# Attention and a gated feed-forward layer on one core: another ending for the last block and newly searched queues

## The chip, the core and the metric

The kernel runs on one core of a Trainium2 chip. TensorE multiplies matrices into PSUM (eight banks of 128 partitions x 512 fp32), VectorE (DVE), ScalarE (ACT) and GpSimd (POOL) work on the elements, and SyncE (SP) issues the DMAs. The engines run side by side, each through a queue of its own, and wait for each other through semaphores. The metric is the device time of one execution in microseconds (us).

## The reference

x is 2048 x 512 in bf16. xn is x with each row normalised; the result is x + attention(xn) + feed-forward(xn):

```python
xn = _layernorm(x)
qkv = (xn @ wqkv)                      # 32 heads of 16
scores = einsum("bhqd,bhkd->bhqk", q, k) * 16 ** -0.5
o = einsum("bhqk,bhkd->bhqd", softmax(scores), v)
A = o.reshape(B, S, D) @ wo
gate, up = xn @ W_gate, xn @ W_up      # 512 -> 1792
B = (gate * (gate > 0) * up) @ W_down
return x + A + B
```

## The kernel before

**Blocks.** The 2048 queries are cut into four blocks of 512 (c4). The 32 heads are taken as four groups of eight (gg), each in two parts of four heads (ee). For each of the 32 triples (c4, gg, ee) the loop goes over 16 key tiles of 128 keys. A head has only 16 dimensions, so TensorE is used in pieces of 64 rows x 32 columns: four matmuls side by side in columns make a *half group* that uses one half of the rows ("row half" 0 or 1), and two half groups of different row halves can run at once. All of these matmuls are recorded at line 250, in `matmul_loaded`.

**Scores, exponentials, P V.** For most key tiles the scores go two half groups at a time, a "score pair", into one of two pairs of banks (0 and 1, 4 and 5), and ScalarE takes the exponential of both banks in one instruction (line 1375, `ring<-ps`, 718 times). For the other key tiles ("quads") the exponential is approximated by integer arithmetic: DVE adds a bias to the scores of each of four banks (line 1330) and makes two shifted copies, by DVE (line 1349) or POOL (line 1345). The products with V ("P V", `ring,v_aug` and `qd,v_aug`) are summed in PSUM over all key tiles of a triple. V has a column of ones, so the sum also gives the softmax's denominator. In all triples but the last both row halves add into one bank, and a half group that follows one of the other half in the same bank waits for it. The remaining four banks (2, 3, 6 and 7, `P_b`) serve P V sums, quads, projections and the feed-forward layer in turn.

**Normalising.** After a triple DVE copies the P V sum to SBUF, the denominators go through three small DMAs and a reciprocal, and POOL multiplies (lines 1237 and 1242); the odd part is packed into the tile of the even part by DMAs (line 1246).

**Feed-forward and output rows.** Between the score pairs TensorE does the projections, the gate and up products and the output rows. `out_rows` makes one tile of 128 output rows: 14 products with W_down, four with wo, and DVE adds the residual x and stores it through SP. For the last block the last two of the four wo products are not ready in time. `out_rows` then sums only the first 16 products, and DVE adds x to them and keeps the sum in fp32 in the space of xnT (line 1061, `resid`).

**The ending** is `normalise_last` (line 1122). For the last triple alone (`LAST2 = 1`) the two row halves of P V add into two banks, so that they need not wait for each other. When both are done, ScalarE copies the one to SBUF (line 1148) and DVE adds the other (line 1150), in two column halves; then DVE transposes (line 1153), takes the reciprocal of the denominators (line 1154), transposes these back (line 1155) and multiplies (line 1157) into `qf`. Meanwhile TensorE computes the products of wo with the two output tiles before the last for all four rows (`stream_out`, in the banks that the scores have left), and for row 3, which stands in `TAIL_ACT`, adds `resid` by an fp32 matmul with the identity (line 1133). Each row then gets its last product, from `qf`. DVE adds `resid` to rows 0 to 2 (line 1174), ScalarE copies row 3 (line 1171), and SP stores all four (line 1179). SP waits for all earlier DMAs ahead of its last `LAST_STORES` stores and for these at the end.

**What sets the order.** The kernel records 8,251 operations and an order of them is written out in `PLAN`, a packed string that a search with a planner has made beforehand: for each place in it which operation comes next, and which buffer each new tile gets. `Graph.run` unpacks it into one queue for each engine, and `Graph.emit` puts in the semaphores. The planner's costs stand in the `G.op` calls; they have no effect on the chip but through that order.

Of the kernel before, what the change touches and what calls it, by code (L numbers as in the profile page):

```python
# [13 lines left out]
ACTF = mybir.ActivationFunctionType  # L14
ALU = mybir.AluOpType

S = 2048
D = 512
H = 32
# [19 lines left out]
LAST_STORES = 4  # L39
# [15 lines left out]
LAST2 = 1  # L55
TAIL_ACT = (3,)
# [65 lines left out]
PLAN_OPS = 8251  # L122
PLAN = (
    "c-n1S1z;3c*PZibve|?P-r(+~K+zK1H53RgAq1zmLkq#JcySHx1oxuBixj8DwYa1-B)jwe``*m#&hq_5vOD|azANXP`<5z-?|)qU;npkhm-SBk%JG0+=1?9OFU$$t_)PpZ9&?`sx#E46{UQBP9-7;D"
    "=UY><D-W!Pig#D;eI!lD@z7?SVte7W#hl8mH{2Y<&EH({?qk_vJk!1JbU6Uxh2039E8-c%vSJ}9=1|2uRL+(k$TwoF?)3*vle5jk`|RXB47Z)yv>w(`bYn$sZK+tBadS6gynJfzO!nxW@#3W%C*Hxc"
    "ndc<Zc%8%A0<@vrlU5V2<p?fc$c16c1<%op4Qx@OC)|n$yk0f-l-r20y6IiHJv_N#`igVzO&o6d%sho*yJ47cl5RRc7|&g*VX%1=V+#)H9wQ*S&tK-YhNrk`mN3eg%&l{apQbZ~&E|n%_{j_vJ#(qL"
    "xrwyPo^@8V%qUxd;I?08&KMgT>sqNt&yBn^?6TZui>Y@5g?kFlc<;5*zK+~aJaj{*h+NNY#aa5(*g{w-=P8~-)6MvEFLIb$nihDA&-_ehT<qkr+8n1d`BZvZymYBzTW0KFd~TjdSf(&ru5s^CVXJcK"
    "RGMu*)0JdZ1cMn-;o>KqQhX#{x|w018>X>t=7zLNF6cIg%lU3$wtPS@nOn@43%E@ix#>g8|Gq~0;-IVnCOjz?7Uwm6&5ivm=ef<Gh!@f-Zfs{5F1%xyXyl3<z|GUjI3+9G&+s;6Qo?k%*ukwBM=-ZF"
    "wi0vQ=0@^k={C=~L}0%7*+JcljEap>JQ;75zaktfgX(6+AF;lhK4hk!6%%y0X9Rc40+Zzk6Aa8vbZ{Fncru?nDJMfNV5}iZg_&S1kL1ByGrEj}jAK^(4QowbTHE=Q1tc6v_lw%0K}im(e9#}$@j9d#"
    "w1``7W~7?P8pEZA>#Z0XhFd3>Kind}xM`)^f<422Yg5yFSjKwT!&aBx^y3~bv%#p1c;rX?KYu03UtvZ{ySZhK=@wz7=_=EcrhB+mMr7-kK$lp~JgB*pfvW%c3kq->Mwr$cCb%V6FuNKc&$!`13DZwr"  # L130
    "KoG_ln8CU7Rl+FD#z<}>V#W}zo7F9oO$Lb@Oy$98-AsF$!u2Gl;)N|w&Jd+=CSh1SW88vP4-c3&$gK^!qXW8CxjO8mDbb31M3{{%%}4O&tBXl1-Cvwv!@ZXVIJb!;?qvrb81igp{cRT^Uiwh%WNcg9"
    "qiuZFv#T|0F!!nti9lYY(CyMkx5-gUs+iDXI@wnIx)<>cZ_2eilq?s6$AhMLfK3b9>*Oo_YVHir@ja)~&EfFTY*xs=QhMe((7jY(LYqAvcI|Cty>3GtYfso5<Pk`UO|bfmvxJ0V-_S$JG6trYG$sll"
    "h2qgzoPVX6y+Jlt5WevHg0E8MD_XX3pGWg@?jxOTTE)_L7EgOnfm>{4(U3)wZtJH&U`xUnU}%)N#a+f8;<3(rgsLDqD~Q&{ZkU8?aFb*<YnBub@F6nYKofW{*VbHdPmvib7-?<DIsvN|hH?{7JhW?!"
    ";T~|em`6g1xt1Y2EtE6i%&a(WE@zzIKrZo?d|;f=l)Y|6F(sg+53YM%PV~jC_?m=fY;8<eEHPy;odt6S|H2rpc#zImSFv%wCI1bE<`z&|OUkj_FxsX2nI`KNLYs>lde#zj+)__wBA8Khd)gOce?!D6"
    "-WE&rN|txIQL@aCTZ$Juy@+byyyER3xYXfB=U_=LuBC9@t$9nq&29aOxA%}81$=5vHy{#Lhhvc|M4Bm3d^%LF*!y0Oru3Z0RQ$G+dnK`z^PU#hI+7VYGjw*KG=-1iZEk$jgGV5Fouhciac?mzwnR~M"
    "PwNU3`xR>qt6{NH5*FGk%2z<j?TxKzgSUg?RySqzGsY-xCM>t|*2f)YV+^k$rmnXT$j$(|oyiUM&_(DtcWE{U+3z|$ROZ9Ewo`E*8uvoF4Z!S|A<9={xDO0@KC!LttpM9eyo_Q2nn}1Y!9mAY*G9TW"
    "4#1OG#v)#KaZevBk>2b(J)B@#=W(h>F(f&doh41LNFL?pe&)*Hw)-d}XJn*3J9vf~lT49kp2#ki$=)P?FWm{L$$dK-#ix1o`PfFB);N1ZY>8~^uE{3Uz4^d>T6sGG+t;wfm0fb#<(iKbc7U-r$=vpo"
    "dm3@WCEUv?rg|40fL&I5FkOcY11zHER<k5A$3sz8S1a3i8?hRCiyPQ%u4qVgPy6fL$O1E1_-3)3hb0ZT<=)1@rXTSCl#}_^twXfo+@Yj+F~s^|Zsny<t0yoa-o$5%tY8N+DMj3t_HtXdZ1&SyTHiu%"
    "&yARQzr;=da_^;<mkxF7R?X;%JtPee(D}Mh_w*MQ{c+E&pA8H=O^=Zl9<^Za2W*PR7fS3&Y5=@(Il_IK4=azDM>AMGr`(;Jj*}6$dUaDc**Mo0An7=h>ukwkiyE_u4AUMvf!J=%cnV_{ohhdFGsKjU"
    ";)+Lf=$`cBp61V_eCw*vWLCMXMs}O`dL{{Zu3W9ev4U!a&$@r`5H`F-CC=xeFxwTQbq#8<w#8nyYe-8;dNhZX1G)*Ba)NGguSaAlU*FgJP?opN@=~rv!2c^CylCVBGhYc|-iTUv)0PypF`bV^+{T6}"  # L140
    "+SkNpmk!+9)Y$LrxSdXXNRs<>jMg@~?+rM&ci6V0amDvr79T@=klafQP`<L;D>FP_S$KOrPh)IAxWTDV{vUerwBPcT=dQtGeb`*4+nC<Q`d&gc?>!8($5&U<y0_uB)xEv;b!%tiX8J2y;^wyq_A5S*"
    "W$?sK_jZxo?t0yP2TNOWZo4n`Dlg+k)&3op&n3xM{LU4xLv{GveOTwyVRJUO-Q#@q6_ocH#rGCnw{A7K_5F>MBC^!2t1)g~eVG^8Ci$5cjn>Vs+um0i;A!=Q%yxmOSeI~&TNktj_>zi}&6Vf&O|fpA"
    "ty^kOZo94Coxx??HhVJKxYe}o#Ke`aX^5pbOqjPIUAI~m?g0zqytc0#yeaMZuFSZbfCtR%z-N73<i&6acHDDSZr$+dibaZ^mPhy82iaOT4+~ffWVR@V%2iCbGnmR~;e41{u{U=f3Q)kkU}q4x`Td^M"
    "xhB*Yt10;ZC8=*K!0j++YnZ@&uETu3KJ~O9%2)Vff9cbC_~ItFe+O#2jDz=EWZ&<8?f7P|GmfvAL9t!SnU`wb!&-1?C5LgdWsDPE{NF}Q@zE+i;A0e@r=o4&+xawDHstobjQyW6#+{12v-=9$^%OrJ"
    "p5WXLdR{cNU-)vLcz?~s_AA@3zht+k3IFQy+2#c$9en?L<bWgPU#O&&SrMqZs_JKpYg)h;RS!tU+fdD4eS&m&lL7u>ct*|b@2205>$$bR7@p>$XMQgFi_uRpAjJKarDyDBZq322;sJer4|##?456PG"
    "QqeXlzf|&ES)8RkaTWDhrIkR=N+&C^y|fDbq+dt^s<Q=USg5W|@4%Kv0VN!FfLsp8M@_uQ=FmR;1BChAep!D{Eth=cOmtpJNvw9H=4&8Rvijzmmk7mK*WQSBt4Hzse`&pb0ZyXcUK|?_Xbi(Av%#}~"
    "Pu=SvatqqVH^!$#_|NMb1ibY-z}fYAz<FFKjZ?2P`~-~prVRF^)!(IM<w^s?TCr7HyYGSiZC!y&R6Y7NtB7MYfOAQj^RtsioJe*$-9G?5TRK+g-IL1#2SS#+Sa(<K1z^`NwGK7-{zo8Q`=#EFT7g?1"
    "0%w~t2O0DyP(auEcPZ3=3L75@Ov%dbWq)#Z2e55k^r{xoK%EwA+Npk8b71AN4l6q?@IM3$DZp+Qxl&Y3-3eIrLfex7jMp-}OAH(ejM(#|7W7v4!$@F0-fn9&3MkeTY<=66H-NG0XY}%4azGmaOiU?t"
    "Ds`f^0_c?a$uNxD0J7%59~~FuoCY-0x+bj}j1uBisf*nML5D9h<=A$Xa~tq|&O3SU<;P~AXqkvn_-$2tQ~;ubSf5cLiLoeoF)u>UCeiUZBvCyJRPfi5aRjKg@?H>9em)FTnufHUk|+JF{tj$+rlCao"
    "_9jV1^5aC;P2EvoI`A6F9a0Le0$My;i(&V&UjjlM)gR@+ok0Eb6<`ngkN?F{lm;a99)l5+-6t#YAp<)AMSf$w=Tt^9@^Q!H!<Uo7_cG}9o&xPt{HI{Zm$mfji^}MXC`#$t!R5d##y|dY1}GmF?OHs4"  # L150
    "A<%sRdY>ugf2KklW!m?3Ci#`vN`}lvCp|!04@5v+-*!shoxo%CoSF)UY5_U!xqF-h9<=Pbd}E~g$3x`6Xss>cW&*p1Yn$Jp{lZ%L{>E`MZg`|J)xZxgvOjV8WqR#m>#HBB7RFr}_N1k!XK-r3Enu=X"
    "SNGRCP&f;^60onzF%)fe6UciK6<r;dINQ$!?mi0?Rg8MT@4fe;){<`5LCeQ1bF5~c5-K0Anm`k>1mntMRDT3y){kTC&d1r|JceJ!G5*V8l6(9m*0KT6rcjQ2(ry*Li*Kn43O+z4?PGD^C^9|S-~CPI"
    "O80=QY<MGFZ#UxXDzR36*WZO*4;Xp%Att_0Q*(W*gRdWFxliLBE?UR5<&+NRkop5I-)g;aLfF%+c)7HlwsZz?@fBvYa<j~sF@ZL?{3!EV>}cntH2YJZ?PMKU`m4zL3@w4?U5X<m3-Aw;t~zcOP=m{j"
    "8HF)jF!v|qe&j|jgtcAUQr{c^+(EV{$iQw^rNP&eg7T{wfgOPhyQRF_(0574MV)E`Eql)Dm(+|3kxuzJ^+!i5+V8dlB`&L+|2v1O=PA-ZKUw7JYP}0>Jx<fxBDt{`{#k3jx;3y<Pu7wG(P&pgY;<M6"
    "=bw(&Ox%?fbg(Z?D9`lo9T?hh4dGVwz-dcv=ezqKWdapGnr-2QihZQOHf#~;ayHV>i4dW1#$(%DtVMa?RQl&o93N<lt=QP=WVl;fH6LXEk-|8(jw)?48a};zl+_?)c>4~g%j4e={dixXX{9zu+_999"
    "b{S$=6<wp3TarqhFL#O%qjjS-(=PqD(eF#)WP;yP8|vvH<&Kx9kW4FovK-TB+i?!G&I&9RA-Y?Dzxp(e0AzE^me??f41bFiEDD5fflW3yXQT6_0Q<0N(y*nSRz6^}DTsey?N9Fz=%fg~>5M^4&F-d1"
    "trK;8t!N)YnWxo`La*Lej3rNv%X{ZcnG3rKn%X<DB>xy7QtLNIhu_ZNMAT_dWKttX<-^Iqb3~W=32g}A4o~Vn=luHCw=ayy6x|uPjmdg>c7}@Z6pmM!REnJ`<vhMeOjyzx<+pq!XpQW8;(9#L<Uj&O"
# [97 lines left out]
class Graph:  # L255
# [124 lines left out]
    def emit(self, nc, es):  # L380
# [93 lines left out]
        def play(e, eng):  # L474
# [953 lines left out]
```

## Time and profile before

| | us |
|---|---|
| median of three runs | 691.45 |
| fastest and slowest run | 690.92, 691.89 |
| profiled execution | 692.29 |
| its span, first to last instruction | 690.4 |
| busy in the span: TensorE, ScalarE, DVE, POOL | 680.9, 670.5, 603.0, 499.3 |
| first exponential starts, last one ends | 11.0, 680.45 |
| granted TensorE clock | 0.998 |

In the profile PE is TensorE, PEld its weight loads, DVE VectorE, ACT ScalarE, SPq SyncE's queue. A row of the timeline gives start, duration, engine, line, operation, what is written and read, shape and count; several like instructions are one row. A row of the stretches gives, for each engine in the order PE, PEld, DVE, ACT, POOL, its busy time and in brackets its instructions; then the granted clock, the DMA engines' busy share and GB/s; the stretches of a single tile show only the engines that touch it. A matmul's row is longer than its share of TensorE, since matmuls overlap.

### The profile page before, as it was taken

To read this page: it belongs to the slowest core of one execution; us is meant where nothing else is said; L and a number is where in the kernel's file an instruction comes from. 1 tells how busy PE (TensorE), PEld (TensorE's weight loads), DVE (VectorE), ACT (ScalarE), POOL (GpSimd) and SP (SyncE) were. 2 spreads that over 40 slices of the span, in tenths; PEclk is the share of its full clock that TensorE was granted. 3 is DMA by queue.
4 is the path that set the end of the run, shared out by engine and by line. 5 is a ranking of instruction groups with operands and counts; after the bars stand their busy time and mean duration, and the time that the engine had idled before them with its cause. 6 is when DMAs were issued, how large, how long until landed. Compare 5 with 4: busy or idle time off the path is not lost.

```text
span 690.4 us, 45217 instructions
## 1 busy us (share of the span) xinstructions
PE 680.9 (99%) x22248; PEld 357.3 (52%) x19848; DVE 603.0 (87%) x1017; ACT 670.5 (97%) x731; POOL 499.3 (72%) x507
## 2 busy tenths in 40 slices
PE   8999999999999999999999999999999999999997
PEld 4455555545545555555444565544554455555463
DVE  9958899999989788999999788989998887988876
ACT  6999999999999999999999999999999999999994
POOL 3223669777788778878677885988878778786791
PEclk9999999999999999999999999999999999999999
DMA  7330121021222021201200022030211013030111
GB/s 214 47 75 21 50 75 52 8 77 52 72 81 56 22 70 31 80 23 28 70 23 26 19 61 73 20 90 6 65 42 33 12 45 95 18 104 23 29 31 59
DMA packets 55941, 35.87 MB, mean 52 GB/s; under 512 B 19336, under 2 KB 51784, under 8 KB 55752
## 3 DMA queue, kind: packets, MB, share of 16 engines
q1 hardware_dynamic: 55752, 32.97, 17.4%
q8 instruction: 165, 2.70, 1.7%
q14 instruction: 24, 0.20, 0.1%
HBM read 26.35 MB, written 2.35 MB: 42 GB/s over the span
## 4 chain that ended last, share of the span: by engine, by line
PE 94%; DVE 4%; issue 1%; DMA 0%; POOL 0%; DVEq 0%
PE ps L250 94%; DVE qd L1330 1%; DVE stats L724 1%; DVE xn_sb L737 1%; DMA x_sb<-in_A_x_dram 0%; DVE hT L1017 0%; DVE qd L1349 0%; DVE xnT L778 0%; POOL rstd L719 0%; PE ps L1133 0%; DVE mv L725 0%; DVE xn_sb L1174 0%; DVE up_sb L1013 0%; DVE kT L866 0%; DVEq L514 0%
## 5 line engine op out<-in xcount | busy, mean ns | idle before, releaser
L1375 ACT ACTIVATE ring<-ps 128x1024 bf16<-128x1024 f32 x718 | 664.0, 1099 | 5.5 <-PE ps L250 4.1
L1345 POOL TENSOR_TENSOR qd<-qd,ints 128x512 int32<-128x512 int32 x446 | 450.0, 1039 | 157.3 <-DVE qd L1349 95.7
L250 PE MATMUL ps<-qT,kT 64*32 64x512 bf16 x8192 | 458.2, 374 | 1.0 <-DVE qd L1330 0.2
L1330 DVE TENSOR_SCALAR qd<-ps 128x512 int16<-128x512 f32 x612 | 397.8, 685 | 55.0 <-PE ps L250 50.5
L250 PE MATMUL ps<-qd,v_aug 64*32 64x512 bf16 x3672 | 267.2, 375 | 0.2 <-issue 0.2
L250 PE MATMUL ps<-ring,v_aug 64*32 64x512 bf16 x2872 | 237.7, 375 | 0.8 <-DVE kT L866 0.6
L1310 PEld LDWEIGHTS <-kT 64*32 64x32 bf16 x7676 | 156.7, 92 | 125.1 <-issue 33.0
L1282 PEld LDWEIGHTS <-v_aug 64*32 64x32 bf16 x4660 | 111.3, 91 | 70.7 <-issue 17.3
L250 PE MATMUL ps<-xnT,wgs 64*32 64x512 bf16 x1792 | 138.1, 374 | 0.3 <-issue 0.2
L250 PE MATMUL ps<-xnT,wus 64*32 64x512 bf16 x1792 | 137.8, 375 | 0.0
L808 PEld LDWEIGHTS <-wgs 64*32 64x32 bf16 x1792 | 43.3, 91 | 32.2 <-issue 8.0
L250 PE MATMUL ps<-Wd,hT 64*32 64x512 bf16 x768 | 57.7, 375 | 0.8 <-DVE qd L1330 0.7
L808 PEld LDWEIGHTS <-wus 64*32 64x32 bf16 x1792 | 43.6, 91 | 28.8 <-issue 6.2
L1349 DVE TENSOR_SCALAR qd<-qd 128x2048 int16<-128x2048 int16 x83 | 56.4, 690 | 1.9 <-PE ps L250 1.7
L808 PEld LDWEIGHTS <-hT 64*32 64x32 bf16 x1792 | 41.7, 92 | 30.1 <-issue 6.4
L250 PE MATMUL ps<-Wv,hT 64*32 64x512 bf16 x512 | 45.2, 375 | 0.0
L250 PE MATMUL ps<-Wk,hT 64*32 64x512 bf16 x512 | 43.5, 375 | 0.0
L1017 DVE SCALAR_TENSOR_TENSOR hT<-ps,up_sb 128x512 bf16<-128x512 f32 x56 | 38.4, 685 | 5.6 <-PE ps L250 5.1
L1013 DVE COPY up_sb<-ps 128x512 f32<-128x512 f32 x56 | 38.4, 685 | 3.3 <-PE ps L250 2.9
L250 PE MATMUL ps<-Wo_p,x_sb 64*32 64x512 bf16 x480 | 39.7, 375 | 0.5 <-issue 0.4
L250 PE MATMUL ps<-xnT,Wq 64*32 64x512 bf16 x480 | 36.0, 374 | 0.0
L250 PE MATMUL ps<-xnT,Wk 64*32 64x512 bf16 x480 | 34.6, 374 | 0.5 <-DVE xnT L778 0.3
(72 smaller groups left out, 266.3 us busy)
## 6 DMA issues: line engine op xcount, KB each, us to landing
rb<-rec_scr SPq DMA_DIRECT2D x31, 256.0 KB
wus<-in_B_W_up_dram SPq DMA_DIRECT2D x38, 128.0 KB, 3.1
wgs<-in_B_W_gate_dram SPq DMA_DIRECT2D x38, 128.0 KB, 3.1
xr_sb<-in_A_x_dram SPq DMA_DIRECT2D x16, 128.0 KB, 2.9
out_dram<-xn_sb SPq DMA_DIRECT2D x16, 128.0 KB, 2.2
qT<-qf SPq DMA_DIRECT2D x120, 16.0 KB, 2.8
x_sb<-in_A_x_dram SPq DMA_DIRECT2D x8, 128.0 KB, 2.4
x_sb<-oT SPq DMA_DIRECT2D x60, 16.0 KB, 2.7
```

Of the source, the lines that this page charges most:

```text
L250: return e.add_instruction(mybir.InstMatmult(name=e.bass.get_next_instruction_name(), engine=mybir.EngineType.PE, ins=[e.lower_ap(x), e.lo ...
L724: G.op("DVE", 580, lambda e, m=m: e.bn_stats(stats[:, m, :], xs(m)), reads=[t_xm[m]], writes=[t_st], prio=pr, order=last_xn if m == 4 else ())
L737: G.op("DVE", 320, lambda e, m=m, t=t_n: e.tensor_scalar(xn_sb[:, t.slot, :], xs(m), mv[:, m, 0:1], rstd[:, m:m + 1], op0=ALU.subtract, op ...
L808: e.ldweights(w()[rows, 32 * j:32 * j + 32], tile_position=(rows.start, 32 * j))
L1013: G.op("DVE", 603, lambda e: e.tensor_copy(up_sb[:, tup.slot, :], bank_of(tu)), reads=[tu], writes=[tup], prio=-590)
L1017: G.op("DVE", 603, lambda e: e.scalar_tensor_tensor(out=hT[:, th.slot, :], in0=bank_of(tg), scalar=0.0, in1=up_sb[:, tup.slot, :], op0=ALU ...
L1282: e.ldweights(vs(j), tile_position=(64 * half, 32 * j))
L1310: e.ldweights(ks(m), tile_position=(64 * half, 32 * m))
L1330: G.op("DVE", 601, lambda e, j=j, tx=tx: e.tensor_scalar(qd[:, tq.slot, 512 * j:512 * j + 512], ps[:, BANK[tx.slot], :], IBIAS[3], 0.0, op ...
L1345: G.op("POOL", POOL_NS / POOL_PIECES + 60, lambda e, x=x, n=n, c=slice(i * m, i * m + m): e.tensor_tensor(x().bitcast(I32)[:, c], raw().bi ...
L1349: G.op("DVE", 600, lambda e, n=n, x=x: e.tensor_scalar(x(), raw(), float(SHIFTS[n + 1]), None, op0=ALU.add), reads=[ti, tq], writes=[t], p ...
L1375: exp_ops[u] = G.op("ACT", 904, lambda e, tr=tr, k0=k0: e.activation(ring[:, tr.slot, :, :], ps[:, 4 * k0:4 * k0 + 2, :], ACTF.Exp, scale= ...
```

## The change

1. `LAST2 = 0`: the last triple's P V sum goes into one bank, like all others. ScalarE's two copies and DVE's two adds go; DVE transposes straight from PSUM, and its multiply reads PSUM too.
2. `TAIL_ACT = (1, 3)`: in the last block rows 1 and 3 are no longer evicted after 16 products. Their banks are kept open to the end ("held"); x is added by one more product, with the bf16 identity as weights. The last three products go into the same bank, and a shared counter (`flags`) gives the first and the last half group their marks in whatever order the queue has them. Rows 1 and 3 come after rows 0 and 2 in the sequence of jobs. The fp32 matmul is gone. Rows 0 and 2 stay as they were, in the two banks of one score pair.
3. At the end ScalarE copies rows 1 and 3 out of PSUM and issues their stores itself, with a semaphore (`stored`) for which SP waits at the very end; SP has the two stores of rows 0 and 2 (`LAST_STORES = 2`).
4. `PLAN` is new as a whole (8,248 operations), from a search whose planner lets TensorE's operations report their ends in the order of its queue. The order of all five queues differs nearly everywhere, also far from the ending.

```diff
-LAST_STORES = 4
+LAST_STORES = 2
-LAST2 = 1
-TAIL_ACT = (3,)
+LAST2 = 0
+TAIL_ACT = (1, 3)
-PLAN_OPS = 8251
+PLAN_OPS = 8248
 PLAN = (
...
+        self.stored = es.enter_context(nc.semaphore("stored"))
...
+                eng.wait_ge(self.stored, 16 * len(TAIL_ACT))
...
             t = tile or Tile("ob", P_b, BGBANKS)
+            held = c4 == NB - 1 and i in TAIL_ACT
...
+            if held:
+                pairs.append((lambda: ident[:], lambda: xr_sb[:, txr.slot, :]))
+                left = [2 * len(pairs) + 6]
+
+                def flags(n=left[0]):
+                    left[0] -= 1
+                    return left[0] == n - 1, left[0] == 0
+                mm_chain(t, pairs, reads + [txr, t_id], pr, slots=slots, flags=flags)
+                kept[i] = t, flags
+                return
...
-            for i in range(4):
+            for i in range(4) if c4 < NB - 1 else sorted(range(4), key=lambda i: i in TAIL_ACT):
...
-            tA, tB = Tile("finA", P_sc, [0]), Tile("finB", P_sc, [1])
-            rows = [(tA, 0), (tA, 1), (tB, 0), (tB, 1)]
+            free = Tile("finA", P_sc, [NU % 2])
+            rows = [(free, 0), (kept[1][0], 0), (free, 1), (kept[3][0], 0)]
...
-                    o = G.op("PE", 860, lambda e, i=i, t=t, sub=sub: e.matmul(bank_of(t, sub), identf[:], resid(i), start=False, stop=False),
...
-                G.op("ACT", 300, lambda e, c=c: e.activation(up_sb[:, tup.slot, c], at_bank(tp)[:, c], ACTF.Copy), reads=[tp],
-                G.op("DVE", 340, lambda e, c=c: e.tensor_tensor(o_sb[:, tos.slot, c], up_sb[:, tup.slot, c], at_bank(tp_hi)[:, c], ALU.add),
-                G.op("DVE", 340, lambda e, c=c: e.transpose(flip(c), o_sb[:, tos.slot, c]), reads=[to], writes=[tt] if h else [tot, tt], joins=[tot] if h else [], prio=-949 + 10 * h)
+                G.op("DVE", 340, lambda e, c=c: e.transpose(flip(c), bank(c)), reads=[tp], writes=[tt] if h else [to, tt], joins=[to] if h else [], prio=-949 + 10 * h)
...
+                G.op("DVE", 340, lambda e, c=c: e.tensor_tensor(qf[:, tl.slot, c], spread(c), bank(c), ALU.mult),
+                     reads=[ts, tp], writes=[tn] if h else [tl, tn], joins=[tl] if h else [], prio=-946 + 10 * h)
...
+                    if i in TAIL_ACT:
+                        G.op("ACT", 566, lambda e, t=t, sub=sub, to_=to_: e.activation(xn_sb[:, to_.slot, :], bank_of(t, sub), ACTF.Copy),
+                             reads=[tf, t], writes=[to_], prio=-900 + i)
+                        G.op("ACT", 100, lambda e, store=store: store(e).then_inc(G.stored, 16), reads=[to_], prio=-890 + i, name="store", lat=1900.0)
+                        continue
```

More of the change, by code (lines that the diff above doesn't have):

```diff
@@ L812, in bass_parallel_sum__mha_block__glu_gated_reglu__prompt_kernel, with mm_chain, counted @@
         chains = [0]
-        def mm_chain(tile, pairs, reads, prio, sub=0, slots=None, mode="half", weights=None):
+        def mm_chain(tile, pairs, reads, prio, sub=0, slots=None, mode="half", weights=None, flags=None):
             n = len(pairs)
             count = [0, n * (2 if mode == "half" else 1)]
-            def flags():
+            def counted():
                 count[0] += 1
                 return count[0] == 1, count[0] == count[1]
+            flags = flags or counted
             made = []
@@ L1144, in normalise_last @@
-            flip = lambda c: o_sb[:, tot.slot, c]
+                    for o in stream_out(t, sub, i, lambda tg=tg, i=i: oT_of(tg)[:, 128 * i:128 * i + 128], wo, [tg], n == 0 and i not in TAIL_ACT, False, NU + 5 + i, i not in TAIL_ACT):
+                        if i not in TAIL_ACT:
+                            o.order |= set(pv_ops[part(keys[-1])][-2:])
+            to, tup, tl = Tile("o", P_o), Tile("up", P_up), Tile("oTl", P_qf)
+            bank, flip, spread = lambda c: ps[:, BANK[tp.slot], c], lambda c: o_sb[:, to.slot, c], lambda c: up_sb[:, tup.slot, c]
@@ L1153, in normalise_last @@
[L1153 removed]
+                tt, tr, ts, tn = (Tile() for _ in range(4))
+                G.op("DVE", 340, lambda e, c=c: e.transpose(flip(c), bank(c)), reads=[tp], writes=[tt] if h else [to, tt], joins=[to] if h else [], prio=-949 + 10 * h)
                 G.op("DVE", 190, lambda e, c=c, h=h: e.reciprocal(rlast[:, 8 * h:8 * h + 8], flip(c)[:, DH - 1:256:32]), reads=[tt], writes=[tr], prio=-948 + 10 * h)
[L1155 to L1156 removed]
@@ L1157, in normalise_last @@
-                G.op("DVE", 340, lambda e, c=c: e.tensor_tensor(oTl()[:, c], o_sb[:, tos.slot, c], up_sb[:, tup.slot, c], ALU.mult),
-                     reads=[ts, to], writes=[tn], joins=[tl], prio=-946 + 10 * h)
+                G.op("DVE", 340, lambda e, c=c, h=h: e.transpose(spread(c), rlast[:, 8 * h:8 * h + 8].unsqueeze(2).to_broadcast([128, 8, 32])),
+                     reads=[tr], writes=[ts] if h else [tup, ts], joins=[tup] if h else [], prio=-947 + 10 * h)
+                G.op("DVE", 340, lambda e, c=c: e.tensor_tensor(qf[:, tl.slot, c], spread(c), bank(c), ALU.mult),
+                     reads=[ts, tp], writes=[tn] if h else [tl, tn], joins=[tl] if h else [], prio=-946 + 10 * h)
@@ L1177, in normalise_last @@
[L1177 to L1183 removed]
+                    tf, to_, m = Tile("fin%d" % i), Tile("ost", P_xn, [i]), 12 + i
@@ L1184, in stream_out @@
+                    G.op("DVE", 603, lambda e, i=i, t=t, sub=sub, to_=to_: e.tensor_tensor(xn_sb[:, to_.slot, :], bank_of(t, sub), resid(i), ALU.add),
+                         reads=[tf, t_res[m]], writes=[to_], prio=-900 + i)
+                    t.r.append(G.ops[-1])
+                    dma(store, 128, reads=[to_], writes=[Tile()], prio=NU + 20, stream=("out", m % 8))
+        def stream_out(t, sub, i, w, wo, reads, start, stop, prio, late=True):
             made = []
             for half in range(2):
-                fn, load = chain_part(w, wo, lambda: bank_of(t, sub), half, lambda first=start and not half, last=stop and half: (first, bool(last)))
+                fn, load = chain_part(w, wo, lambda: bank_of(t, sub), half, kept[i][1] if i in kept else lambda first=start and not half, last=stop and half: (first, bool(last)))
@@ L1187, in stream_out @@
                 new = not t.w
                 o = G.op("PE", 216, fn, reads=reads + [t_wo, t_wol], writes=[t] if new else [], joins=[] if new else [t], prio=prio, mode="half", half=half,
-                         bank=(t, sub), after=NU if start else None, load=load, weights=reads)
+                         bank=(t, sub), after=NU if start and late else None, load=load, weights=reads)
                 if (t, sub) in fin_prev:
```

232 lines of the change are left out of this document (98 added, 134 removed).

## The prediction

> **What bounds the kernel now.** I read the page first, then the stretches, then the timelines of each engine over the last 10 us.
>
> ```profile
> span 690.4 us, 45217 instructions
> ...
> PE 680.9 (99%) x22248; PEld 357.3 (52%) x19848; DVE 603.0 (87%) x1017; ACT 670.5 (97%) x731; POOL 499.3 (72%) x507
> ...
> L1375 ACT ACTIVATE ring<-ps 128x1024 bf16<-128x1024 f32 x718 | 664.0, 1099 | 5.5 <-PE ps L250 4.1
> ...
> L250 PE MATMUL ps<-qT,kT 64*32 64x512 bf16 x8192 | 458.2, 374 | 1.0 <-DVE qd L1330 0.2
> ```
> ```profile
> 11.00:78.00 67.00, 65.49 (x2063) 35.40 (x1970) 53.78 (x103) 65.60 (x72) 22.81 (x30) 1.00 0.32 70
> ...
> 413.00:480.00 67.00, 66.88 (x2288) 34.45 (x2008) 60.05 (x97) 67.00 (x74) 52.71 (x53) 1.00 0.18 52
> ...
> 614.00:680.50 66.50, 66.31 (x2288) 36.99 (x2004) 54.81 (x89) 65.28 (x71) 50.12 (x50) 1.00 0.14 40
> 680.50:690.40 9.90, 6.08 (x126) 1.95 (x106) 5.22 (x14) 1.25 (x3) 0.91 (x1) 0.87 0.17 55
> ```
> ```profile
> 11.00:78.00 67.00, 21.92 (x260) 65.60 (x71) 1.00 0.32 70
> ```
> ```profile
> 675.74 4.71 ACT L1375 ACTIVATE ring<-ps 128x1024 bf16<-128x1024 f32 x5
> 681.09 0.66 ACT L1148 ACTIVATE up_sb<-ps 128x256 f32<-128x256 f32 x2 [0.63 <-PE ps L250]
> 687.01 0.60 ACT L1171 ACTIVATE xn_sb<-ps 128x512 bf16<-128x512 f32 x1 [5.26 <-PE ps L250]
> ```
>
> TensorE and ScalarE run side by side and hold each other up. The 718 exponentials end at 675.74 + 4.71 = 680.45. The stretch from 413 to 480 us holds 74 of them, 0.905 us each, without idle time; the first stretch (71 of its ScalarE instructions are exponentials, by the stretches of ring alone) needs 67/71 = 0.944, the last one 66.5/71 = 0.937. So (680.45 - 11.0)/718 = 0.932 us is the mean over the middle, and 718 x (0.932 - 0.905) = 19 us are lost there, all told. Whatever the change does to TensorE's queue can give back at most these 19 us. The other 9.9 us after the last exponential are a chain of small steps:
>
> ```profile
> 680.54 0.67 PE L250 MATMUL ps<-ring,v_aug 64*32 64x512 bf16 x12
> 681.14 0.41 PE L250 MATMUL ps<-Wo_p,x_sb 64*32 64x512 bf16 x4
> 681.18 0.38 PE L250 MATMUL ps<-ring,v_aug 64*32 64x512 bf16 x4
> 681.61 1.32 PE L250 MATMUL ps<-Wo_p,x_sb 64*32 64x512 bf16 x24
> ...
> 683.60 1.12 PE L1133 MATMUL ps<-xnT,identf 128*128 128x512 f32 x2
> 684.66 0.39 PE L250 MATMUL ps<-Wo_l,x_sb 64*32 64x512 bf16 x4
> 684.69 0.38 PE L250 MATMUL ps<-Wo_l,qf 64*32 64x512 bf16 x4
> 684.88 0.38 PE L250 MATMUL ps<-Wo_l,x_sb 64*32 64x512 bf16 x4
> 685.40 1.56 PE L250 MATMUL ps<-Wo_l,qf 64*32 64x512 bf16 x28
> ```
> ```profile
> 679.96 0.68 DVE L1061 TENSOR_TENSOR xnT<-ps,xr_sb 128x512 f32<-128x512 f32 x1
> 681.63 0.75 DVE L1150 TENSOR_TENSOR o_sb<-up_sb,ps 128x256 f32<-128x256 f32 x2 [0.99 <-PE ps L250]
> 682.30 0.44 DVE L1153 STREAM_TRANSPOSE o_sb<-o_sb 128x256 f32<-128x256 f32 x1
> 682.77 0.20 DVE L1154 RECIPROCAL rlast<-o_sb 128x8 f32<-128x8 f32 x1
> ...
> 683.22 0.40 DVE L1155 STREAM_TRANSPOSE up_sb<-rlast 128x256 f32<-128x256 f32 x1
> ...
> 683.65 0.43 DVE L1157 TENSOR_TENSOR qf<-o_sb,up_sb 128x256 bf16<-128x256 f32 x1
> 684.00 0.44 DVE L1155 STREAM_TRANSPOSE up_sb<-rlast 128x256 f32<-128x256 f32 x1
> 684.47 0.42 DVE L1157 TENSOR_TENSOR qf<-o_sb,up_sb 128x256 bf16<-128x256 f32 x1
> 685.82 1.89 DVE L1174 TENSOR_TENSOR xn_sb<-ps,xnT 128x512 bf16<-128x512 f32 x3 [0.93 <-PE ps L250]
> ```
> ```profile
> L1179 SPq DMA_DIRECT2D out_dram<-xn_sb x4: 332/338/430, 686.6 to 688.1; - x4
> ...
> DMA to landing us min/median/max: 1.7/1.7/1.8
> ```
>
> The last P V group starts at 681.18 and what waits for it (DVE at 681.63, TensorE at 681.61) starts 0.43 us later: that is the price of a handover between row halves. DVE then works alone until 684.89 (both halves of qf), the first half being ready at 684.08, but TensorE is still in the fp32 matmul until 684.72 and takes it up at 684.69. Rows 0 to 2 leave through DVE from 685.82 to 687.71, row 3 through ScalarE until 687.61, but its store is issued at 688.1, behind row 2's on SP's queue. It lands about 1.8 us later, at 689.9.
>
> **The change part by part, the ending.** All times here are on the clock of before, with the last exponential at 680.45.
>
> 1. P V in one bank. In the new queue the last ring group of row half 0 stands behind nine groups of its half since the last score pair (seven before), and the waits for the packed output tile now stand among them. That makes 2 x 0.215 and up to half a microsecond of semaphore waits; I let it start at 680.9 instead of 680.54. Then row half 1 must wait for it, because both halves now add into one bank: +0.43, and five P V groups follow in series, four spacings of 0.215, the last reported 0.43 later. DVE begins at 680.9 + 0.43 + 0.86 + 0.43 = 682.6, 1.0 later than before. Best case 682.2 (no backlog), worst 683.2 (a second handover).
>
> 2. The DVE chain loses the ScalarE copies (0.66, under other work) and both adds. Two transposes, two reciprocals, then transpose, multiply, transpose, multiply: before, qf's first half came 684.08 - 682.30 = 1.78 after the first transpose and the second 2.59 after it. The operand now lies in PSUM; the nearest row that reads PSUM at this size, the add at L1150, gives 0.75 for two, against 0.43 for the multiply that reads SBUF, so I price both alike. qf is ready at 684.4 and 685.2, that is 0.3 later than before in both halves.
>
> 3. TensorE under that chain. The fp32 matmul (1.12) is gone; four half groups that add the residual by the identity come (two for each kept row, 2 x 0.215 per row half). Behind the last score pair the queue now holds 60 half groups where it held 42 and the fp32 matmul; 18 were moved there, 9 x 0.215 = 1.9 us per half. From the last P V start (682.2) eleven groups of row half 1 remain before qf is asked for, 2.4 us and some handovers: 684.7, so TensorE, not DVE, still lets the first qf group start at about the old 684.69. If this cover were longer, each group would cost 0.215.
>
> 4. The rows. Row 0 and 2 go through DVE, 1 and 3 through ScalarE, alternating. Row 0's second group follows one handover later, with two others between: its sum is there at 685.55 (before 685.80). Row 2 needs the second half of qf (685.2, start 685.4), a handover and a report: 686.25. Row 3 is last in the queue behind three groups of its half: 686.9. ScalarE takes 0.60 for it, to 687.5, and issues its store itself at 687.6 instead of SP's 688.1. Landing after 1.7 to 1.8: 689.4 instead of 689.9. DVE ends at 686.95, so row 2's store (landing 688.7) is not last.
>
> The ending gives -0.5. No DMA issued by ScalarE is in the trace. Its bounds are the landings of all stores of the output, from the view of that tensor:
>
> ```profile
> DMA to landing us min/median/max: 1.7/2.2/4.5
> ```
>
> The nearest are the four late stores at 1.7 to 1.8, on idle DMA engines as here; so I take 1.75. With the worst P V start (+0.6) and the slowest landing (+2.7) the ending costs 2.8; with the best start and no handovers left it gives 1.2. SP waits for all but its own two stores during the DVE chain and ends with one more wait for ScalarE's stores; the waits lie under the chain, and the last adds less than the 0.5 us that already follows the last landing.
>
> **The change part by part, the middle.** The order of all queues is new, from the first microseconds on; the work is the same (2,766 half groups per row half before, 2,768 after), less two DVE residual adds (L1061, 0.68 each). So I counted the queues as built.
>
> - Between two score pairs ScalarE allows 0.905 us, four groups per half (0.86) but not five (1.08). Intervals with five or more go from 111 to 105, in the last tenth from 14 to 11, which is the work moved to the end. Price of one: between 0 and 1.08 - 0.905 = 0.17; six fewer give 0 to -1.0.
> - Waits of one row half for the other at three places or less behind the awaited group: 139 before, 116 after. A place is about 670/5,650 = 0.12 us, three are 0.36, the handover 0.43; so 23 fewer save 0 to 0.1 each for most, 0 to -2.3.
> - The distances of scores to the exponential that frees their bank, and to the DVE work, are nearly the same.
>
> I take -1.2 for the middle, a little over a third of the -3.3, since ScalarE can only use what arrives at its score pairs. On the other side nothing in the counts says that the new order is worse, but a window of the old order ran at 0.937 where others ran at 0.905; were the whole middle so, it would cost 718 x 0.005 = 3.6.
>
> How the row halves start matters for all of this:
>
> ```profile
> 36.87 0.38 PE L250 MATMUL ps<-qd,v_aug 64*32 64x512 bf16 x4
> 36.88 0.38 PE L250 MATMUL ps<-Wv,xnT 64*32 64x512 bf16 x4
> 37.09 0.38 PE L250 MATMUL ps<-qd,v_aug 64*32 64x512 bf16 x4
> ...
> 37.30 0.38 PE L250 MATMUL ps<-qd,v_aug 64*32 64x512 bf16 x4
> ```
>
> In the queue all three qd groups (one half, 0.215 apart) stand ahead of the Wv group of the other half, yet this starts second. Starts run ahead by some groups. Ends are reported in order: the qf group that started at 684.69 is asked for by the one that starts at 685.40, 0.71 later and not 0.43, because the group of 684.88 stood ahead of it in the queue. The Trainium skill, page "TensorE: Matmul & The Clock Gate", section "The mechanism" in Part 3, has matmuls strictly first in, first out, in their starts and their ends; the trace agrees for the reported ends and contradicts it for the starts, and the sum goes by the trace.
>
> Sum: 692.29 (the profiled execution: span 690.4 and 1.9 around it) - 0.5 - 1.2 = 690.6. That execution stands 0.84 over the median of 691.45, so the forecast against the runs is 689.7.
>
> **The rivals.**
>
> A. Starts in queue order. Were they, a group behind one of its own half would leave the other half empty. Laid out so, the order before fills 3,100 steps of 0.215 and the new one 3,075: 25 x 0.215 = -5.4, and -0.5 for the ending: 685.6. For it: the change is to the order itself, and 19 us are there to take. Against: 36.88 above; with two groups of lead allowed, both orders come out equal to 0.1 us. The skill's rule named above would give this time.
>
> B. Slower: the score pairs of the new order come late to ScalarE, in the middle. Place: the semaphore waits of TensorE's queue, where a wait stops both halves; the new order moves nearly every one of its 5,650 groups. Price: the last window's rate, +3.6, less 0.5: 694.5. It decides from the point where the mean distance of exponentials exceeds 0.935 us (+1.9, which outweighs the ending's 0.5). For it: the windows differ that much with the same code. Against: all counts point slightly the other way.
>
> C. No difference: the ending's -0.5 is eaten by the later P V sum (worst start +0.6) and the middle stays. 691.4.
>
> **How the numbers follow.** 0.2% of 691.45 is 1.4 us, about what a measurement can tell from no change. My forecast (half of the chances, own range 687.5 to 691) is faster in four parts of five and within 0.2% in the rest: 0.40 and 0.10. A has 0.12, all faster. B has 0.25, of which 0.22 slower. C has 0.13, the same. Together: faster 0.52, same 0.26, slower 0.22. The range goes from 686.5 (most of A is out) to 693.3 (into B).
>
> **What would show it.** Right: exponentials at 0.930 us on average and the last one about 1 us earlier; after it 9.4 us instead of 9.9; DVE starting its transposes some 2.2 us after the last exponential (1.2 before for the add); first qf group at 4.2 us after it; the last store ScalarE's, landing 1.7 to 1.8 after its issue. Wrong: idle time before ScalarE's exponentials over 20 us in sum; a P V sum that ends more than 2.7 us after the last exponential; a ScalarE store that takes over 2.5 us; or a mean distance at 0.925 or less, which would be A's sign.

## The result, and the profile after

The changed kernel takes 686.5 us (median, 685.28 to 689.76) where the kernel before, run beside it, takes 691.24 (690.09 to 691.89). The ratio is 0.9938, with a 95% interval from 0.992 to 0.9956: 4.3 us less, between 3.0 and 5.5. The forecast was 689.7 us in a range from 686.5 to 693.3, so the time lies at the range's lower edge, 3.2 us below the forecast. Both steps of the forecast were wrong in size: the ending was to give 0.5 us and gave nothing, the middle was to give 1.2 and gave all of it.

The profiled execution takes 686.07 us. Its page, the lines that answer to those of before:

```profile
span 684.2 us, 45020 instructions
...
PE 675.6 (99%) x22262; PEld 345.9 (51%) x19654; DVE 598.5 (87%) x1012; ACT 666.8 (97%) x730; POOL 499.8 (73%) x507
...
L1365 ACT ACTIVATE ring<-ps 128x1024 bf16<-128x1024 f32 x718 | 660.4, 1141 | 2.9 <-PE ps L250 2.5
```

The work is the same. TensorE's busy time and the idle time ahead of the exponentials are smaller. The stretches, in the columns of before (PE, PEld, DVE, ACT, POOL):

```profile
11.00:78.00 67.00, 66.33 (x2123) 33.71 (x2022) 54.79 (x105) 66.66 (x74) 24.29 (x32) 1.00 0.32 69
413.00:480.00 67.00, 66.97 (x2269) 34.22 (x2000) 60.86 (x100) 66.98 (x74) 52.72 (x52) 1.00 0.15 40
614.00:674.25 60.25, 59.68 (x2056) 31.47 (x1768) 49.40 (x81) 60.23 (x66) 45.14 (x45) 1.00 0.13 39
674.25:684.20 9.95, 6.98 (x216) 3.32 (x180) 3.90 (x11) 1.19 (x2) 1.27 (x1) 0.96 0.18 57
```

The first stretch holds 74 ScalarE instructions where it held 72; the middle one is unchanged. The last exponential ends at 674.25 (680.45 before), and from there to the end it is 9.95 us (9.96 before). So next to nothing was won behind the last exponential. The exponentials themselves, counted by stretch, in before and after (the stretches of the tile ring; columns: length, TensorE's P V products that read ring, then the exponentials under ACT):

```profile
11.00:110.00 99.00, 33.90 (x400) 97.34 (x105) 1.00 0.29 66
110.00:540.00 430.00, 152.96 (x1864) 427.99 (x465) 1.00 0.17 46
540.00:673.00 133.00, 45.99 (x540) 131.21 (x142) 1.00 0.16 46
```
```profile
11.00:110.00 99.00, 34.47 (x416) 98.66 (x108) 1.00 0.28 66
110.00:540.00 430.00, 152.66 (x1868) 427.44 (x466) 1.00 0.17 46
540.00:673.00 133.00, 47.27 (x568) 132.98 (x146) 1.00 0.17 48
```

Three more exponentials (2.7 us at 0.905) in the first 99 us, one in the next 430 us, four in the last 133. Part of the last figure is probably chance: the kernels below with moved handovers and with joined pairs, whose order is nearly that of before, show 145 there. The profiled execution of before is also 0.84 us over its median, so the 6.2 us between these two traces are more than the 4.3 us between the kernels.

The ending of after, DVE, ScalarE and the stores:

```profile
676.94 0.78 DVE L1151 STREAM_TRANSPOSE o_sb<-ps 128x256 f32<-128x256 f32 x2 [2.67 <-PE ps L250]
...
678.32 0.42 DVE L1155 TENSOR_TENSOR qf<-up_sb,ps 128x256 bf16<-128x256 f32 x1
...
679.13 0.42 DVE L1155 TENSOR_TENSOR qf<-up_sb,ps 128x256 bf16<-128x256 f32 x1
```
```profile
680.88 0.37 ACTq L1162 DMA_DIRECT2D out_dram<-xn_sb  x1
681.35 0.60 ACT L1164 ACTIVATE xn_sb<-ps 128x512 bf16<-128x512 f32 x1 [0.51 <-PE ps L250]
681.98 0.34 ACTq L1162 DMA_DIRECT2D out_dram<-xn_sb  x1
```
```profile
DMA to landing us min/median/max: 1.7/1.8/2.0
```

And TensorE, from the last score pair on:

```profile
672.74 0.38 PE L250 MATMUL ps<-xr_sb,ident 64*32 64x512 bf16 x4
673.46 0.41 PE L250 MATMUL ps<-Wo_p,x_sb 64*32 64x512 bf16 x4 [0.34 <-issue]
673.51 0.38 PE L250 MATMUL ps<-Wd,hT 64*32 64x512 bf16 x4
673.67 0.41 PE L250 MATMUL ps<-ring,v_aug 64*32 64x512 bf16 x4
...
675.18 0.41 PE L250 MATMUL ps<-ring,v_aug 64*32 64x512 bf16 x4
...
679.05 0.59 PE L250 MATMUL ps<-Wo_l,qf 64*32 64x512 bf16 x8
```

The first Wo_p group (row 1's product with the packed output tile) carries 13 semaphore waits, and it starts 0.72 us after the group ahead of it in its half, which is 0.51 more than the usual spacing of 0.215; the profile shows 0.34 of it as idle time of the whole engine. The last ring group comes at 675.18, 0.93 us after the last exponential. DVE starts its transposes at 676.94.

### The profile page after: what moved, and what is told of

It reads as the page before. It is cut to its first block, busy times and chain, and to the rows that moved or that the text cites. A ratio compares the mean times of both kernels' runs of the same rounds, so it can differ in the third digit from the quotient of the medians.

```text
span 684.2 us, 45020 instructions
## 1 busy us (share of the span) xinstructions
PE 675.6 (99%) x22262; PEld 345.9 (51%) x19654; DVE 598.5 (87%) x1012; ACT 666.8 (97%) x730; POOL 499.8 (73%) x507
## 3 DMA queue, kind: packets, MB, share of 16 engines
q8 instruction: 164, 2.69, 1.6%
## 4 chain that ended last, share of the span: by engine, by line
PE 75%; ACT 18%; DVE 5%; issue 1%; DMA 0%; POOL 0%; ACTq 0%
PE ps L250 75%; ACT ring L1365 18%; DVE stats L726 1%; DVE qd L1320 1%; DVE xn_sb L739 1%; DVE v_aug L876 0%; DMA x_sb<-in_A_x_dram 0%; DVE qT L952 0%; DVE mv L727 0%; ACT xn_sb L1164 0%; DVE qd L1339 0%; DVE xnT L780 0%; POOL rstd L721 0%; DVE xnT L1075 0%; DVE kT L869 0%
## 5 line engine op out<-in xcount | busy, mean ns | idle before, releaser
L250 PE MATMUL ps<-qT,kT 64*32 64x512 bf16 x8192 | 448.7, 374 | 1.3 <-DVE qd L1320 0.4
L250 PE MATMUL ps<-qd,v_aug 64*32 64x512 bf16 x3672 | 263.0, 375 | 1.1 <-issue 0.9
L1300 PEld LDWEIGHTS <-kT 64*32 64x32 bf16 x7584 | 151.1, 92 | 126.6 <-issue 32.6
L1272 PEld LDWEIGHTS <-v_aug 64*32 64x32 bf16 x4544 | 108.7, 91 | 75.6 <-issue 20.4
L250 PE MATMUL ps<-xnT,wus 64*32 64x512 bf16 x1792 | 136.4, 374 | 0.0
L810 PEld LDWEIGHTS <-hT 64*32 64x32 bf16 x1792 | 40.2, 92 | 28.2 <-issue 4.2
```

Of the source, the lines that this page charges most:

```text
L250: return e.add_instruction(mybir.InstMatmult(name=e.bass.get_next_instruction_name(), engine=mybir.EngineType.PE, ins=[e.lower_ap(x), e.lo ...
L810: e.ldweights(w()[rows, 32 * j:32 * j + 32], tile_position=(rows.start, 32 * j))
L1272: e.ldweights(vs(j), tile_position=(64 * half, 32 * j))
L1300: e.ldweights(ks(m), tile_position=(64 * half, 32 * m))
```

## The experiments

Two theories stood against each other. *Order*: the gain is the new order of the middle alone. *Ending*: the order can be looser because the new ending takes work out of the last stretch (18 half groups moved behind the last score pair, two DVE adds gone). All edits of order below move operations in the written-out order and leave everything else as it is.

**The changed kernel again**, to stand beside three of the others.

> The changed kernel once more, unedited, so that it stands beside the three others on one chip. Both theories: 0.9938 of the kernel before, between 0.992 and 0.9956, as measured.

685.26 us, ratio 0.9941 (0.9923 to 0.9959). From the last exponential to the end 9.88 us.

**The order without the ending, and the ending without the order.** The first pair was joined at the 660th exponential:

```diff
 before.py
-PLAN: order of before
+PLAN: order of after up to score pair 660, from there the order of before (buffers renamed to fit)
```

> The kernel before, ending and all, but with the changed kernel's order of work for everything up to the 660th exponential; from there on the order of before. Order theory (the gain is the order of the middle, and the ending is worth nothing): the two traces stand about 5.1 us apart at the 660th exponential (4.67 at the 648th, 5.51 at the 672nd), so 691.2 - 5.1 = 686.1 us, between 685.2 and 687.2. Ending theory (the order can be looser because the ending takes work out of the last stretch): the gain does not come over, 690.5 to 691.5 us.

> The mirror image: the changed kernel, new ending and all, but with the order of before up to the 660th exponential. Order theory: only what the traces gained behind the 660th exponential is left, 6.2 - 5.1 = 1.1 us, so 691.2 - 1.1 = 690.1 us, between 689.3 and 691.2. Ending theory: as the changed kernel, 686 to 687.5 us.

689.02 us, ratio 0.9991 (0.9982 to 0.9999), and 694.97 us, ratio 1.0072 (1.006 to 1.0084). Taken as they are, both numbers speak against the order theory. The trace of the first shows why they can't be taken so. Up to the 660th exponential it runs 5.13 us ahead of the profile of before (after: 5.36). Behind the seam ScalarE stands still twice (timeline of ScalarE), and TensorE's waits in the same stretch name GpSimd:

```profile
625.80 6.60 ACT L1375 ACTIVATE ring<-ps 128x1024 bf16<-128x1024 f32 x7 [1.26 <-PE ps L250]
633.74 2.85 ACT L1375 ACTIVATE ring<-ps 128x1024 bf16<-128x1024 f32 x3 [1.34 <-PE ps L250]
```
```profile
PE ps L250 <- POOL qd L1345: 2.4, 2, 1.5
```

At that place 16 operations stand on different sides of the cut in the two orders, a quad's shifted copies on GpSimd among them, so the joined order has them late. The pair was repeated with a cut at the 633rd exponential, where only two DMA issues differ:

> The kernel before with the changed kernel's order up to the 633rd exponential, joined where only two of the 8,251 steps stand on different sides of the seam (both DMA issues; at the 660th it was 16 steps, GpSimd's pieces of a row group among them, and the trace lost 2.8 us right behind the seam). Order theory: what the traces had gained by there, 4.35 of 6.27 us, 69% of the whole gain of 4.3 us, so 3.0 us less than before (ratio 0.9957, between 0.994 and 0.9975). Ending theory: no gain, ratio 0.999 to 1.001.

> The changed kernel with the order of before up to the 633rd exponential, the same clean seam. Order theory: the 31% of the gain that came behind that point, 1.3 us less than before (ratio 0.998, between 0.9965 and 1.0). Ending theory: all of the gain, ratio 0.9938.

686.89 us, ratio 0.9956 (0.994 to 0.9972), and 687.95 us, ratio 0.9979 (0.9968 to 0.9989). Both fall on the order theory's numbers (0.9957 and 0.998), and the ending theory's lie outside both intervals. The exponentials by stretch, of the first and of the second:

```profile
11.00:110.00 99.00, 34.34 (x412) 98.38 (x107) 1.00 0.27 65
```
```profile
11.00:110.00 99.00, 33.71 (x400) 97.33 (x105) 1.00 0.27 67
```

The early gain goes with the order, not with the ending. Of the whole, 0.0044/0.0062 or some 70% comes ahead of the 633rd exponential without any part of the new ending. The other 30% comes with the new ending and the order around it, but ahead of the last exponential: the tail is 9.96 us in the one and 9.98 in the other. Which of the two earns those 30% these runs don't tell.

**Parted score pairs.** In before 40 score pairs have another half group between their two halves in TensorE's queue; in after two have.

```diff
 before.py, TensorE's queue, at 40 places
  score pair, row half 0
-  P V (or other) group, row half 0
  score pair, row half 1
+  P V (or other) group, row half 0
```

> The kernel before with its 40 parted score pairs joined: the second half of each goes right behind the first, ahead of the group that stood between. Theory of the late report: 1.7 us less, 689.5 us, between 688.7 and 690.5. Rival (reports do not wait): no difference, 691.2 us within 0.5.

688.32 us, ratio 0.9979 (0.997 to 0.9988): 1.4 us less, against 1.7 expected. The opposite edit, in the changed kernel:

> The changed kernel with 130 score pairs pulled apart: the half group of the same row half that stood right behind the pair is put between its two halves, everything else as it was. In before 40 pairs stood so, 16 of them with an exponential that started late, 1.7 us of idle time in all; in the changed kernel two. Theory of the late report (the end of the second half is reported only when the group queued ahead of it has ended): 1.7 us / 40 x 130 = 5.5 us more, 692 us, between 689.5 and 696; the score's start to the exponential's start grows from 0.44 to about 0.65 us at these places. Rival (an end is reported when it happens, whatever stands ahead in the queue): the same pieces of work one place on, 686.5 us, within 0.7 either way, and the distance stays 0.44.

687.67 us, ratio to before 0.9963 (0.995 to 0.9976), which is 0.0022 to 0.0025 or 1.6 us above the changed kernel, with intervals that overlap a little; not 5.5, and by the time alone nearer to the rival's number. The trace decides between the two. One such place, exponential 220 (counted from 0, here and below), first in the repeat of the changed kernel (score pair on TensorE, then its exponential), then parted:

```profile
214.06 0.46 PE L250 MATMUL ps<-qT,kT 64*32 64x512 bf16 x8
...
214.60 1.12 ACT L1365 ACTIVATE ring<-ps 128x1024 bf16<-128x1024 f32 x1
```
```profile
214.99 0.48 PE L251 MATMUL ps<-qT,kT 64*32 64x512 bf16 x8
215.30 0.38 PE L251 MATMUL ps<-ring,v_aug 64*32 64x512 bf16 x4
...
215.74 1.02 ACT L1366 ACTIVATE ring<-ps 128x1024 bf16<-128x1024 f32 x1
```

Both halves of the pair start together, within 0.1 us, in both (one row of eight matmuls). The group put between is queued ahead of the second half but starts 0.2 us after it, and the exponential starts 0.75 us after the pair instead of 0.54. So the report waits for the group queued ahead. It is so at all such places: from the start of a pair's second half to the raising of its semaphore it takes 0.61 us in the median at the 132 parted pairs of this kernel and at the 40 of before, and 0.43 at all other pairs. In the whole traces of before and after, none of the 3,211 and 3,229 reports of half groups comes out of the order of the queue, although 659 and 542 half groups start more than 0.02 us ahead of one that is queued in front of them.

The commonest distance of two exponentials is 0.904 us. Counted against that, 68 exponentials start more than 30 ns late at parted pairs, by 7.6 us in all; the second half's start lies 0.65 us ahead of them in the median, and 0.46 ahead of the late ones elsewhere. Yet all the lateness together is 15.5 us, against 14.4 in the repeat of the changed kernel: the late ones elsewhere fall from 85 with 11.5 us to 37 with 5.4. What is lost at one place is for the most part saved at the next. The mechanism is shown; its price in time is a fifth of what the single places show.

**Handovers between the row halves.** This was the larger term of the forecast's middle.

```diff
 before.py, TensorE's queue, at 94 places (one to three places each)
  group A, row half 0, bank b
- group B, row half 1, bank b      (waits for A)
  group C
  group D
+ group B, row half 1, bank b
```

> The kernel before with 94 half groups moved by one to three places so that handovers of a bank between the row halves stand further apart: those three places or less behind the group they follow fall from 139 to 53, of them two places or less from 26 to 10. By the stall that the trace of before shows at each distance (335, 269, 85, 32 and 16 ns at 1 to 5 places) that takes 8.5 us of stalls from one row half or the other. Handover theory: between 0.18 and 0.32 of such a stall reached the exponentials in the two traces (5.5 of 30.0 us in before; 2.8 of the 8.8 that went), so 1.5 to 2.7 us less than before, ratio 0.9961 to 0.9978. Rival (the other half fills in, and the gain was in the waits on VectorE's work and the weights' transfers): ratio 0.999 to 1.001.

> The kernel before with its 40 parted score pairs joined and the handovers moved apart, both. If the two causes are separate, the sum of b_join (0.9979) and the run with the handovers alone: 0.994 to 0.9957, which would be most or all of what the changed kernel gains (0.9938 and 0.9941). If the handovers are worth nothing, 0.998.

> The changed kernel with the two late waits of the ending moved as in a_tail, its last two parted score pairs joined, and 81 half groups moved so that handovers at three places or less fall from 116 to 38. Handover theory: 5.4 us of stalls less by the distances, 0.18 to 0.32 of that, and 0.2 us of the ending: 1.2 to 1.9 us less than the changed kernel, ratio to before 0.991 to 0.9925. Rival: as the changed kernel, 0.9935 to 0.9945.

689.8 us, ratio 1.0006 (0.9996 to 1.0016); 688.0 us, 0.9989 (0.9979 to 0.9998); 685.37 us, 0.9946 (0.9931 to 0.996), no different from the changed kernel. The handover theory falls in all three. In the trace of the first, the time by which half groups start later than 0.215 us behind the group ahead of them in their half, put down to the wait that ended last, went from 36.1 to 30.8 us for waits on the other row half, but from 31.9 to 35.7 for waits on ScalarE. So a good part of what was taken away returned as waits on ScalarE; why the rest was worth nothing is not shown. The second run also repeats the joining of the pairs: against the first of these three it gains 0.0017, about as much as the joining gained alone (0.0021).

**The semaphore waits in the ending.**

```diff
 after.py, TensorE's queue, behind the last score pair
- row 1 x packed tile, half 0      (13 waits)
  ... P V groups of the last triple
- row 3 x packed tile, half 0
  last P V group
+ row 1 x packed tile, half 0      (13 waits)
+ row 3 x packed tile, half 0
```

> The changed kernel with the first product of row 1 with the attention output, and that of row 3, moved behind the last P V group: the wait for 13 semaphores (TensorE stands 0.72 us, 672.74 to 673.46) is then behind the P V sum and not ahead of it. Path theory (the ending hangs on the P V sum and the transposes): the first transpose 2.1 instead of 2.69 us after the last exponential, the end 9.3 to 9.4 instead of 9.94 after it, 0.5 us less than the changed kernel. Rival (TensorE is full from the last exponential to the last row group, so the wait costs the same wherever it stands): the first transpose comes earlier, the first row group that needs it still starts 4.8 us after the last exponential and the end stays at 9.9, no difference within 0.2 us.

685.23 us, ratio to before 0.9937 (0.9918 to 0.9956). DVE, TensorE's first qf group and ScalarE's last copy, with the last exponential ending at 673.88:

```profile
676.00 0.78 DVE L1151 STREAM_TRANSPOSE o_sb<-ps 128x256 f32<-128x256 f32 x2 [2.10 <-PE ps L250]
```
```profile
678.44 0.59 PE L250 MATMUL ps<-Wo_l,qf 64*32 64x512 bf16 x8
```
```profile
680.74 0.60 ACT L1164 ACTIVATE xn_sb<-ps 128x512 bf16<-128x512 f32 x1 [0.51 <-PE ps L250]
```

(The last row is the second of two copies.) The transposes come 2.12 us after the last exponential, as the path theory had it, but the first qf group only at 4.56 (4.80 in after, 4.71 in its repeat), the last copy at 6.86 (7.10, 7.03), and the end at 9.69 (9.95, 9.88). Half a microsecond ahead of DVE became 0.2 at the end, and the time can't be told from that of the changed kernel: the rival is nearly right in the number. It is not right in the reason. At its new place the group with the 13 waits (the second row) starts 0.23 us after the group ahead of it in its half, so there the waits hold nothing:

```profile
675.27 0.38 PE L250 MATMUL ps<-Wv,hT 64*32 64x512 bf16 x4
...
675.50 0.41 PE L250 MATMUL ps<-Wo_p,x_sb 64*32 64x512 bf16 x4
```

Other waits took back half of it. The ring group that took the moved group's old place starts 0.18 us late, and row half 1 stands 0.30 us for row 1's bank, which the moved group has only just used. Of the 1.21 us that row half 0 is held between the last score pair and the first qf group, 0.96 are left.

**Who stores.**

```diff
 after.py
-LAST_STORES = 2
+LAST_STORES = 4
-                eng.wait_ge(self.stored, 16 * len(TAIL_ACT))
-                        G.op("ACT", 100, lambda e, store=store: store(e).then_inc(G.stored, 16), ...)
+                        dma(store, 128, reads=[to_], writes=[Tile()], prio=NU + 20, stream=("out", m % 8))
```

> The changed kernel with rows 1 and 3 stored by SyncE instead of by ScalarE, as in before; ScalarE still takes them out of PSUM. By the prediction's step (in before the store was issued 0.5 us behind the end of ScalarE's copy, in the changed kernel 0.03): the end 0.45 us later, 10.3 to 10.4 us after the last exponential, ratio to before 0.9945 to 0.995. Rival (the landing or the closing of the queues hides it): the end stays at 9.9, ratio 0.9938 to 0.9941.

686.12 us, ratio 0.9955 (0.9941 to 0.9969). The interval overlaps the changed kernel's, so the time alone shows no difference. In the trace the end is 10.12 us after the last exponential, 0.2 later and not 0.45. All four stores now stand on SP's queue:

```profile
L1160 SPq DMA_DIRECT2D out_dram<-xn_sb x4: 338/432/452, 680.6 to 682.0; - x4
```

SP issues the last one 0.25 us after ScalarE's copy ends (681.16 + 0.60), where ScalarE needs 0.03. But ScalarE, free of issuing row 1's store (0.37 us), takes row 3 at 6.95 instead of 7.03 to 7.10, 0.02 us after TensorE's report instead of 0.10.

## Why the prediction came out as it did

The size of the gain lay at the edge of the range, and that was luck: 686.5 us is outside the forecast's own range (687.5 to 691), and the range's lower edge was set with rival A in view, whose mechanism is excluded below. The reasons were mostly not those given.

*Step 1, P V in one bank.* Mis-sized. The last ring group of row half 0 was to start 0.45 us after the last exponential and started at 0.93. The step named two more groups (0.43) and "up to half a microsecond of semaphore waits", but let the group start at 680.9, which doesn't even hold the two groups (680.54 + 0.43 = 680.97). The waits came out at their upper bound, 0.51 us, and nothing had been put in for them. DVE began at 2.69 (2.60 in the repeat) instead of 2.15, still within the bounds given (1.75 to 2.75). The experiment that moved these waits gave 2.12.

*Step 2, the DVE chain.* Right: qf's halves were ready 678.74 - 676.94 = 1.80 and 2.61 us after the first transpose (forecast 1.78 and 2.59). Reading PSUM costs the multiply nothing (0.42).

*Step 3, TensorE under the chain.* Right in kind: TensorE, not DVE, lets the first qf group start, and in after it works without a pause from the last exponential to the last row group (6.98 us busy; 6.08 before). It came at 4.80 instead of 4.25 us, and that is step 1's delay carried on: the last P V group starts at 2.26 instead of 1.75, and the eleven groups behind it take 2.54 where "2.4 us and some handovers" was said. Moving the waits helped so little because TensorE sets this start: the first qf group comes 0.64 us after its half of qf is ready there (678.44 against 677.80).

*Step 4, the rows.* ScalarE takes row 3 at 7.10 instead of 6.45 and issues its store at once, which lands in 1.7 us as assumed. The issue by ScalarE was priced at 0.5 and is worth 0.2. With step 3's delay the ending is 9.95 where 9.4 was forecast: the ending's -0.5 is 0.

*The middle.* The forecast's term for the handovers (0 to -2.3) measured nothing: 1.0006 with 86 fewer close ones in the order of before. (TensorE's queue has 5,570 operations and not 5,650, which leaves a place at 0.12 us.) The shorter count of five-group intervals was not tried apart. The term that was missing is the parted score pairs. The prediction had the mechanism, read from 684.69 and 685.40 (ends are reported in order), and applied it only to the ending; it did not count in the queues how often a group stands between the two halves of a pair, 40 times against two. Item 4 of the change had named this very rule as what is new in the planner. Joining the pairs in the order of before gave 1.4 of the 4.3 us; at the rate of the parted kernel, 1.6 us for 130, it would be only 0.5, so their share of the gain is known no closer than that.

A second piece is visible without an experiment of its own. In TensorE's waits from 30 to 40 us of before:

```profile
PE ps L250 <- DVE kT L866: 0.6, 1, 0.6
PE ps L250 <- DVE v_aug L873: 0.2, 1, 0.2
```

TensorE stands 0.6 us for DVE's copy of a key tile, and exponential 26 starts 0.68 us late. All six kernels with the early order of before show this wait, at 0.5 or 0.6 us; in all that have the new one the same view has no row. It disappears with the order, but nothing here moved it alone. What is left, 2.3 us or more, is spread over many holds of a few tenths of a microsecond, and its cause stays open. The terms that the forecast named for the middle could give 3.3 us at most, and the larger of them, up to 2.3, gave nothing.

*Rivals.* A gave 685.6 us and the distance of exponentials is 0.924 (663.3/718), beyond the 0.925 that was named as A's sign. Its mechanism is nonetheless excluded by the rows of after quoted above: the ring group of 673.67 stands in the queue ahead of the Wd group of the other half that starts at 673.51. The sign was badly chosen, since any large gain in the middle brings the distance there. The Trainium skill, page "TensorE: Matmul & The Clock Gate", section "The mechanism" in Part 3, has matmuls first in, first out, in their starts and their ends. The parted pair's rows agree for the ends, at 0.75 against 0.54 us, and the rows at 673.51 and 673.67 contradict it for the starts. B (slower) and C (no difference) did not come: idle time ahead of the exponentials fell.

## What to carry to other kernels

Count in the built queue, and not only in time, what stands between the two halves of anything that another engine waits for: here a group in between put the report off by 0.18 us in the median, though both halves had started together. A stall that is visible in a trace is worth its length only if nothing else holds the engine right behind it; with TensorE at 99% and ScalarE at 97%, stalls on one row half of TensorE, taken away by the dozen, returned in good part as waits on ScalarE and gave no time. Where two long orders are joined to see which part earns a gain, cut where the same work has been done in both, and read the seam in the trace before the verdict.

## What had not been expected

- One group's 13 semaphore waits put its start 0.51 us off right behind the last score pair, and nothing (0.23 us after the group ahead, where 0.215 is usual) a few microseconds later in the queue. Of the half microsecond won, 0.2 was left at the end.
- Parting 130 score pairs made 7.6 us of late starts and cost about 1.6 us of time, by intervals that overlap a little.
- A seam at which 16 of 8,251 operations were out of place cost 2.8 us in one kernel and about 5 in its mirror image, through GpSimd's copies arriving late.
- Executions of one and the same order differ by single pauses of TensorE for which the trace names no releaser ("issue"). In after exponential 429 is held by 1.04 us; in the repeat it is held by 0.49, and exponential 306 by 0.82, which in after isn't held at all. These nearly cancel (663.3 and 663.8 us from the first exponential to the end of the last); the microsecond by which the two profiles differ lies ahead of the first exponential, which starts at 10.92 and 11.89 us. Two profiles a microsecond apart need not differ in anything that the code does.
